# First batch's first 120 rows of scores gathered from an SBUF tile, and blocks of 120, 110, 110 and 108 rows

## The chip, the core and the metric

The kernel runs on one core of a Trainium2 chip. The metric is device microseconds (us) of one execution. Before the change it is 876.28 us, the median of three runs (875.92 to 877.65). The core has the engines that the profile calls PE (TensorE, matrix products; PEld is its weight load), DVE (VectorE), ACT (ScalarE), POOL (GpSimd) and SP (SyncE), which here issues every DMA. SBUF is the on-chip memory, PSUM the banks that PE writes to, DRAM the memory that DMAs reach outside the core.

## The reference

Attention in which the heads are mixed before and after the softmax, followed by a feed-forward layer:

```
q, k, v: (4 batches, 12 heads, 448 rows, 64)   w_pre, w_post: (12, 12)
scores = (q @ k.T) / 8                          # per batch and head, 448 x 448
scores = einsum('bhij,hg->bgij', scores, w_pre) # heads mixed
attn   = exp(scores - max_j);  attn /= (sum_j + 1e-9)
attn   = einsum('bhij,hg->bgij', attn, w_post)  # heads mixed again
x      = (attn @ v) as (1792, 768)
out    = (x@w_in * sigmoid(1.702 * x@w_in)) @ w_out   # w_in 768 x 2048, w_out 2048 x 768
```

## The kernel before

**Attention.** For each batch the scores of a head, 448 rows by 448 columns, are made in four blocks of 112 rows (`QI`). A product (`qk`, L292) leaves one head's block in a PSUM bank, rows on partitions. ACT or DVE copies it to a staging tile `sc` (L327) that holds two heads, and one DMA (L331) sends the pair to the DRAM tensor `sd` of its batch and block, laid out as row, head, column. Six such sends make a block.

The mixing of heads wants the twelve heads of a row on twelve partitions. So the work goes on in 45 steps per batch, a step being ten rows: `gather` (L368) reads ten rows by twelve heads from `sd` into the 120 partitions of a tile `r`, and one product with a block-diagonal matrix `wa` mixes the heads (`mx`, L380). DVE takes the maximum (`nm`, L398), ACT the exponentials and their sum (`e`, L408), POOL and DVE the inverse sum (`rs`, L419 and L424), POOL scales the second mixing matrix (`wr`, L439), PE mixes again and transposes (`pp`, L449), and ACT copies the result to the tile `p` (L503), which holds twelve steps' rows. After twelve steps (the last time nine) `context` multiplies `p` with v (`av`). Batches 0 and 1 do this in float32, batches 2 and 3 with pairs of float16, where a step has two gathers of five rows, each to 60 partitions.

A block of 112 rows does not end where a step ends. The steps 11, 22 and 33 of a batch take rows of two blocks and have a DMA for each. There are four tiles `r`: a gather is issued four steps ahead, when the product of four steps before has freed its tile.

**Feed-forward.** The weights come as 64-bit words, are turned to pairs of float16 on DVE and ACT (L597 to L663, tiles `w`, `w_f`, `w_p`), kept in DRAM (`wd`) and fetched again for each of 32 units (`wt`, L676). The products are `h` (L688) and `po` (L726). They can begin when the first batch's attention is done.

**What sets the order.** The start is written out: six loads of q and k, three of the mixing matrices, then the twelve products of block 0. Of this block the first 64 rows of each pair are sent first, the gathers of the steps 0 to 3 follow, and then the other 48 rows. Its staging tiles are borrowed from places that other tiles use later (`sc`, `g`, `acc`). Everything behind that is ordered by a planner (`add`, `run_all`): a list of tasks with engines, durations, due times and the buffers that they take, from which the order on each engine is written out when the program is built. Each engine, SP too, works through its own list strictly in order. The lines `free.update`, `lanes` and `READY` tell the planner when the engines and the first gathers are free. A DMA's completion is counted on one of eight semaphores in turn, so the ninth DMA waits until the first has landed.

Of the kernel before, what the change touches and what calls it, by code (L numbers as in the profile page):

```python
# [9 lines left out]
F32 = mybir.dt.float32  # L10
# [9 lines left out]
B, H, S, D = 4, 12, 448, 64  # L20
QK16 = (False, False, True, True)
MIX16 = (False, False, True, True)
# [3 lines left out]
GI = 10  # L26
GPB = -(-S // GI)
GPC = 12
CI = GI * GPC
NCH = -(-S // CI)  # L30
QI = 112
KG = GI * H
HI = GI // 2
GAP = 64
# [10 lines left out]
def attention_then_feed_forward(ctx, tc, q, k, v, w_pre, w_post, w_in, w_out, out):  # L45
# [223 lines left out]
        return i0, min(CI, S - i0)  # L269

    def block(c):
        return c * QI, QI

    sd = {}
    for b in range(B):
        for c in range(NCH):
            shape, kind = ([H, 2, S], F16) if MIX16[b] else ([H, S], F32)
            sd[b, c] = dram.tile([block(c)[1]] + shape, kind, name=f"sd_{b}_{c}", tag=f"sd_{b}_{c}")

# [46 lines left out]
        n = block(c)[1]  # L326
        (nc.scalar.copy if eng == "A" else nc.vector.tensor_copy)(t[:n, x, :], two[x][:n, :S])  # L327

    def send_scores(b, c, pr, t, lo=0, hi=QI):
        hi = min(hi, block(c)[1])  # L330
        nc.sync.dma_start(out=sd[b, c][lo:hi, 2 * pr:2 * pr + 2, :], in_=t[lo:hi])  # L331


    def blocks_of(g):
        i0, n = rows_of(g)
        return range(i0 // QI, (i0 + n - 1) // QI + 1)

    def rows_of(g):
        return g * GI, min(GI, S - g * GI)
# [12 lines left out]
    def gather(i):  # L352
        b, g = steps[i]
        i0, n = rows_of(g)
        if MIX16[b]:
            t = flow.tile([128, 2, S], F16, name=f"r_{i}", tag="r", bufs=NRB)
            form = "i h t j -> (i h) t j"
        else:
            t = flow.tile([KG, S], F32, name=f"r_{i}", tag="r", bufs=NRB)
            form = "i h j -> (i h) j"  # L360
        for first, last, at in halves(i):
            if MIX16[b] and g % 2:
                at = GAP - at
            for c in blocks_of(g):
                lo, hi = max(i0 + first, c * QI), min(i0 + last, c * QI + QI)
                if lo < hi:
                    at_lo = at + (lo - i0 - first) * H
                    nc.sync.dma_start(  # L368
                        out=t[at_lo:at_lo + (hi - lo) * H],
                        in_=sd[b, c][lo - c * QI:hi - c * QI].rearrange(form),  # L370
                    )
        row["r", i] = t

    def mix(i):
# [115 lines left out]
    def mixed_to(i):  # L490
        b, g = steps[i]
        n = rows_of(g)[1]
        c, off = g // GPC, (g % GPC) * GI
        if off == 0:
            shape, kind = ([CP, 2, NR, H, CI], F16) if POST16[b] else ([CP, NR, H, CI], F32)
            st["p", b, c] = mixed.tile(shape, kind, name=f"p_{b}_{c}", tag="p")
        p = st["p", b, c]
        if not POST16[b]:
            return p.rearrange("p r h i -> p (r h) i")[:, :, off:off + n]
        return p.rearrange("p t r h i -> p t (r h) i")[:, :, :, off:off + n]  # L500
# [462 lines left out]
        )  # L963

    tags = [("gen", 8)]*3
    homes = [("sc", 3), ("g", 2), ("sc", 3), ("g", 2), ("sc", 3), ("acc", 1)]
    kept = []
    FRONT = 64
    for pr in range(NPAIR):
        two = scores(0, 0, pr, tags[pr % 3])  # L970
        kept.append(scores_home(0, 0, pr, homes[pr]))
        for x in range(2):
            keep_scores(0, 0, x, kept[pr], two, "AD"[x])
        send_scores(0, 0, pr, kept[pr], 0, FRONT)
    nc.vector.tensor_tensor(
        w_mix,
        wrep[:, 0, :].unsqueeze(1).to_broadcast([KG, GI, H]),
# [2 lines left out]
    )  # L980
    mixing(0)
    mixing_pair()
    for i in range(AHEAD):
        gather(i)
    for pr in range(NPAIR):
        send_scores(0, 0, pr, kept[pr], FRONT)


    free.update({"PE": 12.7, "A": 13.3, "D": 16.1, "G": 3.0, "SP": 20.5})
    DMA["free"] = 22.2  # L990
    lanes.extend([19.0, 19.7, 20.4, 21.1, 21.6, 22.2, 22.7, 23.3, 23.8, 24.4])
    READY, LATER = [19.0, 19.7, 20.4, 21.1], 24.4
    held["sc"] = [21.6, 22.7, 23.8]
    held["gen"] = [12.0, 12.2, 12.4, 12.6, 12.8, 12.9, 13.2, 13.5]
    held["g"], held["acc"] = [22.2, 23.3], [24.4]
    r_home = {i: [] for i in range(N)}
    held["r"] = [r_home[i] for i in range(AHEAD)]
    e_home = {i: [] for i in range(N)}
    p_home = {(b, c): [] for b in range(B) for c in range(NCH)}
    x_home = {b: [] for b in range(B)}  # L1000
    acc_home = {b: [] for b in range(B)}
# [198 lines left out]
    for b in range(B):  # L1200
        for c in range(NCH):
            if (b, c) == (0, 0):
                continue
            base = GPB * b + c * QI // GI
            for pr in range(NPAIR):
                x = base - (18 if c == NCH - 1 else 17) + 2 * pr if c else base - 11 + pr
                if b == 0 and (c == 1 or (0, c, pr) in NEAR):
                    x = 0
                x -= (2 if c else 1) * (pr % 2) * (b > 0 or c > 1)
                at_scores.setdefault(max(x, 0), []).append((b, c, pr))  # L1210
# [18 lines left out]
    for i in range(N):  # L1229
        if i + AHEAD < N:  # L1230
            b, g = steps[i + AHEAD]
            n = i + AHEAD
            gathers[n] = add("SP", 0.8 if MIX16[b] else 0.4, lambda n=n: gather(n), [j for c in blocks_of(g) for j in sends.get((b, c), [])], i,
                             size=0.229, takes=[("r", r_home[n])], behind=gathers.get(n - 1))
            if (g + 1) * GI > FRONT and n < GPC:
                gathers[n]["from"] = LATER
        step_tasks(i)
        for what, b, x, *name in at.pop(i, []):
            if what == "whole-kq":
                for n in range(THIRDS):  # L1240
                    for m in "kq":
                        inputs[m, b, n] = whole_load(m, b, n, x + 4 * n)
            elif what == "whole-v":
                loads = [whole_load("v", b, n, x + 2 * n) for n in range(THIRDS)]
                inputs.update({("v", b, n): j for n, j in enumerate(loads)})
                size_tasks("v", b, loads, x + 2, [in_home["v", b, n] for n in range(THIRDS)])
            elif what == "size":
                both = [staged_load(name[0], b, n, "a", x + n) for n in range(THIRDS)]
                size_tasks(name[0], b, [j for j, _ in both], x + 2, [h for _, h in both])
            elif what == "split":  # L1250
                split_tasks(name[0], b, x)
                if name[0] == "q":
                    mixers[b] = add("D", 0.3, lambda b=b: mixing(b), [sized["k", b], sized["q", b], split], x)
            else:
                conversion_tasks(b % 2, b // 2, x)
        for b, c, pr in at_scores.pop(i, []):
            score_tasks(b, c, pr, i)
        b, g = steps[i]
        if g == GPB - 1 or g % GPC == GPC - 1:
            context_tasks(b, g // GPC, i)  # L1260
# [116 lines left out]
```

## Time and profile before

| what | value |
|---|---|
| median of three runs | 876.28 us (875.92 to 877.65) |
| the profiled execution | 875.12 us, span 873.4 us from first to last instruction |
| PE, DVE, ACT, POOL busy | 96%, 73%, 70%, 39% of the span |
| mean granted clock of PE | 0.992 of full speed |
| DMA | 195.64 MB on SP's queue; 225 GB/s on the mean |

The profile is of one execution. Busy time is the time that instructions of an engine ran; a wait is told with what ended it. The windows view gives, for a stretch of the span, the busy time of each engine with the number of its instructions, the clock that PE was granted, the mean busy share of the core's 16 DMA engines and the GB/s that they moved. A share a little above 1 means that packets of one engine overlapped. In the timeline, neighbouring instructions of one group are merged: "x4" are four, and the second number is the time from the first's start to the last's end. A product in float32 is two instructions or more, so one `mx` reads "x2".

### The profile page before, as it was taken

Reading aid. Unit: us, or ns where it says so; the run is one execution under the profiler, and the core shown is the slowest. Engines: PE = TensorE matmul, PEld = TensorE weight load, DVE = VectorE, ACT = ScalarE, POOL = GpSimd, SP = SyncE. Lnnn points to the kernel's source line nnn. Section 1 sums busy time; section 2 is a strip of 40 time slices with the busy share of each in tenths; the row PEclk is TensorE's granted clock in tenths of the full one; section 3 lists DMA queues with packets and bytes.
Section 4 is the critical chain, followed back from the end, with each engine's and each line's share of the span. In section 5 each row is a group of like instructions: output and inputs, shape, how many; then the busy total and the mean of one; then the engine's idle time right before and its main releaser. Section 6 shows DMA issues by size and latency. Waiting matters only on the chain. (4 is left out here: it accounts for less than half of the span.)

```text
span 873.4 us, 20042 instructions
## 1 busy us (share of the span) xinstructions
PE 840.4 (96%) x7300; PEld 515.2 (59%) x7300; DVE 633.3 (73%) x1493; ACT 615.5 (70%) x1373; POOL 340.2 (39%) x529
## 2 busy tenths in 40 slices
PE   8869999999999999989999989999999999999998
PEld 4546756666576666645656546655656566555554
DVE  3657786997979999999878968779786863332323
ACT  4778888896887897967797777677776764324432
POOL 0212332231215632585457634545455553204332
PEclk9989999999999999999999999999999999999999
DMA  7998999999998997777787576587563423252322
GB/s 242 298 288 272 348 297 305 324 341 320 317 341 273 302 315 224 242 225 270 246 278 229 171 252 193 160 231 224 163 202 105 160 80 110 88 189 77 145 86 87
DMA packets 68375, 196.92 MB, mean 225 GB/s; under 512 B 9684, under 2 KB 34516, under 8 KB 68276
## 3 DMA queue, kind: packets, MB, share of 16 engines
q1 hardware_dynamic: 68276, 195.64, 69.4%
q8 instruction: 58, 0.95, 0.4%
q14 instruction: 41, 0.34, 0.1%
HBM read 138.98 MB, written 56.62 MB: 224 GB/s over the span
## 5 line engine op out<-in xcount | busy, mean ns | idle before, releaser
L688 PE MATMUL h<-x,wt 128*128 128x448 f16 x1152 | 246.1, 353 | 0.0
L726 PE MATMUL po<-g,wt 128*128 128x448 f16 x1152 | 240.1, 354 | 3.9 <-ACT e L408 2.9
L726 PEld LDWEIGHTS <-wt 128*128 128x128 f16 x1152 | 110.9, 98 | 101.2 <-issue 7.8
L688 PEld LDWEIGHTS <-wt 128*128 128x128 f16 x1152 | 108.7, 98 | 102.0 <-issue 14.8
L419 POOL TENSOR_SCALAR rs<-sm 120x1 f32<-120x1 f32 (+1 forms) x180 | 52.0, 289 | 275.2 <-ACT e L408 269.3
L398 DVE TENSOR_REDUCE nm<-mx 120x1 f32<-120x448 f32 (+1 forms) x180 | 110.2, 615 | 25.1 <-PE mx L380 15.2
L472 POOL TENSOR_TENSOR a<-w,a 124x448 f16<-124x448 f32 (+1 forms) x90 | 96.1, 1067 | 45.9 <-POOL rs L419 14.5
L449 PEld LDWEIGHTS pp<-wr,e 120*112 120x112 f32 x720 | 84.6, 177 | 36.8 <-issue 19.0
L754 POOL TENSOR_TENSOR acc<-acc,pt 128x448 f32<-128x448 f32 x56 | 65.4, 1169 | 103.9 <-ACT pt L748 96.9
L707 DVE SCALAR_TENSOR_TENSOR th<-th,h 128x448 f32<-128x448 f32 x64 | 39.4, 617 | 86.5 <-ACT th L703 85.7
L380 PE MATMUL mx<-r,wa 120*120 120x448 f32 x180 | 85.3, 564 | 11.0 <-DMA r<-sd 10.0
L449 PE MATMUL pp<-wr,e 120*112 120x120 f32 x720 | 90.4, 269 | 5.1 <-POOL wr L439 4.0
L750 DVE SCALAR_TENSOR_TENSOR acc<-po,ct,acc 128x448 f32<-128x448 f32 x112 | 75.5, 678 | 17.9 <-PE po L726 17.5
L408 ACT ACTIVATE e<-mx,nm,c 124x448 f32<-124x448 f32 (+1 forms) x90 | 65.4, 728 | 24.9 <-DVE nm L400 20.9
L458 POOL TENSOR_SCALAR w<-e,rs 124x448 f32<-124x448 f32 (+1 forms) x90 | 63.5, 706 | 40.4 <-DVE rs L424 29.0
L466 ACT ACTIVATE a<-e,rs 124x448 f16<-124x448 f32 (+1 forms) x90 | 60.3, 672 | 14.7 <-DVE rs L424 14.6
L408 ACT ACTIVATE e<-mx,nm 120x448 f32<-120x448 f32 (+1 forms) x90 | 57.2, 636 | 17.1 <-DVE nm L398 12.8
L748 ACT ACTIVATE pt<-po,ct 128x448 f32<-128x448 f32 x56 | 35.4, 635 | 46.5 <-PE po L726 46.0
L511 DVE TENSOR_TENSOR p<-pp,p 112x480 f16<-112x480 f32 (+1 forms) x90 | 58.2, 648 | 13.7 <-ACT p L507 13.5
L703 ACT ACTIVATE th<-h,ct 128x448 f32<-128x448 f32 x64 | 40.5, 633 | 35.9 <-PE h L688 35.6
L485 PE MATMUL pp<-wp,a 124*112 124x120 f16 x360 | 63.5, 220 | 1.9 <-ACT e L408 1.1
L507 ACT CAST p<-pp 112x480 f16<-112x480 f32 (+1 forms) x90 | 50.6, 562 | 20.4 <-PE pp L487 19.3
(144 smaller groups left out, 1499.0 us busy)
## 6 DMA issues: line engine op xcount, KB each, us to landing
wt<-wd SPq DMA_DIRECT2D x64, 768.0 KB
sd<-sc SPq DMA_DIRECT2D x90, 392.0 KB
r<-sd SPq DMA_DIRECT2D x170, 105.0 KB
r<-sd SPq DMA_DIRECT2D x82, 210.0 KB
w<-in_moe_w_in_dram SPq DMA_DIRECT2D x24, 512.0 KB
w<-in_moe_w_out_dram SPq DMA_DIRECT2D x24, 512.0 KB
wd<-w_p SPq DMA_DIRECT2D x16, 768.0 KB
out_dram<-acc SPq DMA_DIRECT2D x24, 224.0 KB
```

Of the source, the lines that this page charges most:

```text
L380: nc.tensor.matmul(mx[:K, :S], st["wa"][:K, :K], r[:K, :], start=True, stop=True)
L398: nc.vector.tensor_reduce(nm[:K], row["mx", i][:K, :S], axis=AX.X, op=ALU.max, negate=True)
L408: nc.scalar.activation(e[:K], row.pop(("mx", i))[:K, :S], AF.Exp, bias=row.pop(("nm", i))[:K, 0:1], scale=st["c", b][:K, 0:1] if MIX16[b] ...
L449: nc.tensor.matmul(pp[:CP, jc * w:(jc + 1) * w], e[:K, jc * CP:(jc + 1) * CP], columns(i, wr), start=True, stop=True,)
L458: nc.gpsimd.tensor_scalar(w[:K], e[:K], row["rs", i][:K, 0:1], 1.0, op0=ALU.mult, op1=ALU.mult)
L466: nc.scalar.activation(a1[:K], row["e", i][:K], AF.Copy, scale=row["rs", i][:K, 0:1])
L472: nc.gpsimd.tensor_tensor(a2[:K], row.pop(("w", i))[:K], row["a1", i][:K], op=ALU.subtract)
L485: nc.tensor.matmul(o, a1[:K, js], columns(i, wp1), start=True, stop=False)
L688: nc.tensor.matmul(h, w[:, i, c, fc * 128:(fc + 1) * 128], x[:, j, c, :], start=(n == 0), stop=(n == len(terms) - 1),)
L726: nc.tensor.matmul(po, w[:, j, fc, e * 128:(e + 1) * 128], g[:, i, fc, :], start=(n == 0), stop=(n == len(terms) - 1),)
L750: nc.vector.scalar_tensor_tensor(a, po, c, a, op0=ALU.mult, op1=ALU.add)
L754: nc.gpsimd.tensor_tensor(a, a, st.pop(("pt", u, e)), op=ALU.add)
```

## The change

The tile `near`, 120 partitions by 12 heads by 448 columns, takes the copies of the first batch's block 0, which is now 120 rows long. Nothing of it goes to DRAM. The first twelve steps gather from `near`: step g takes the rows g, g+12, g+24 and so on, ten rows from ten partitions, so the rows of a step are not neighbours any more, and `mixed_to` puts a step's results in every twelfth column of `p`. `near` is of the kind `p`, of which there are two. All batches have blocks of 120, 110, 110 and 108 rows, which begin and end where steps do, so no step has rows of two blocks. The front and late parts of the first block's sends are gone, and the borrowed staging tiles with them. The planner's opening numbers are others.

```
@@ -28,7 +28,8 @@
 GPC = 12
 CI = GI * GPC
 NCH = -(-S // CI)
-QI = 112
+BLOCKS = ((0, 120), (120, 110), (230, 110), (340, 108))
+QI = 120
 KG = GI * H
 HI = GI // 2
 GAP = 64
@@ -269,11 +270,11 @@
         return i0, min(CI, S - i0)
 
     def block(c):
-        return c * QI, QI
+        return BLOCKS[c]
 
     sd = {}
     for b in range(B):
-        for c in range(NCH):
+        for c in range(b == 0, NCH):
             shape, kind = ([H, 2, S], F16) if MIX16[b] else ([H, S], F32)
             sd[b, c] = dram.tile([block(c)[1]] + shape, kind, name=f"sd_{b}_{c}", tag=f"sd_{b}_{c}")
 
@@ -326,14 +327,13 @@
         n = block(c)[1]
         (nc.scalar.copy if eng == "A" else nc.vector.tensor_copy)(t[:n, x, :], two[x][:n, :S])
 
-    def send_scores(b, c, pr, t, lo=0, hi=QI):
-        hi = min(hi, block(c)[1])
-        nc.sync.dma_start(out=sd[b, c][lo:hi, 2 * pr:2 * pr + 2, :], in_=t[lo:hi])
-
-
-    def blocks_of(g):
-        i0, n = rows_of(g)
-        return range(i0 // QI, (i0 + n - 1) // QI + 1)
+    def send_scores(b, c, pr, t):
+        n = block(c)[1]
+        nc.sync.dma_start(out=sd[b, c][:, 2 * pr:2 * pr + 2, :], in_=t[:n])
+
+
+    def block_of(g):
+        return max(c for c in range(NCH) if BLOCKS[c][0] <= g * GI)
 
     def rows_of(g):
         return g * GI, min(GI, S - g * GI)
@@ -361,14 +361,15 @@
         for first, last, at in halves(i):
             if MIX16[b] and g % 2:
                 at = GAP - at
-            for c in blocks_of(g):
-                lo, hi = max(i0 + first, c * QI), min(i0 + last, c * QI + QI)
-                if lo < hi:
-                    at_lo = at + (lo - i0 - first) * H
-                    nc.sync.dma_start(
-                        out=t[at_lo:at_lo + (hi - lo) * H],
-                        in_=sd[b, c][lo - c * QI:hi - c * QI].rearrange(form),
-                    )
+            c = block_of(g)
+            lo = i0 - BLOCKS[c][0]
+            if (b, c) == (0, 0):
+                nc.sync.dma_start(out=t, in_=st["near"][g::GPC])
+            else:
+                nc.sync.dma_start(
+                    out=t[at:at + (last - first) * H],
+                    in_=sd[b, c][lo + first:lo + last].rearrange(form),
+                )
         row["r", i] = t
 
     def mix(i):
@@ -495,6 +496,8 @@
             shape, kind = ([CP, 2, NR, H, CI], F16) if POST16[b] else ([CP, NR, H, CI], F32)
             st["p", b, c] = mixed.tile(shape, kind, name=f"p_{b}_{c}", tag="p")
         p = st["p", b, c]
+        if (b, c) == (0, 0):
+            return p.rearrange("p r h i -> p (r h) i")[:, :, g::GPC]
         if not POST16[b]:
             return p.rearrange("p r h i -> p (r h) i")[:, :, off:off + n]
         return p.rearrange("p t r h i -> p t (r h) i")[:, :, :, off:off + n]
@@ -963,15 +966,13 @@
         )
 
     tags = [("gen", 8)]*3
-    homes = [("sc", 3), ("g", 2), ("sc", 3), ("g", 2), ("sc", 3), ("acc", 1)]
-    kept = []
-    FRONT = 64
+    near = st["near"] = mixed.tile([CI, H, S], F32, name="near", tag="p")
     for pr in range(NPAIR):
         two = scores(0, 0, pr, tags[pr % 3])
-        kept.append(scores_home(0, 0, pr, homes[pr]))
         for x in range(2):
-            keep_scores(0, 0, x, kept[pr], two, "AD"[x])
-        send_scores(0, 0, pr, kept[pr], 0, FRONT)
+            (nc.scalar.copy if x == 0 else nc.vector.tensor_copy)(near[:, 2 * pr + x, :], two[x][:CI, :S])
+    for i in range(AHEAD):
+        gather(i)
     nc.vector.tensor_tensor(
         w_mix,
         wrep[:, 0, :].unsqueeze(1).to_broadcast([KG, GI, H]),
@@ -980,22 +981,18 @@
     )
     mixing(0)
     mixing_pair()
-    for i in range(AHEAD):
-        gather(i)
-    for pr in range(NPAIR):
-        send_scores(0, 0, pr, kept[pr], FRONT)
-
-
-    free.update({"PE": 12.7, "A": 13.3, "D": 16.1, "G": 3.0, "SP": 20.5})
-    DMA["free"] = 22.2
-    lanes.extend([19.0, 19.7, 20.4, 21.1, 21.6, 22.2, 22.7, 23.3, 23.8, 24.4])
-    READY, LATER = [19.0, 19.7, 20.4, 21.1], 24.4
-    held["sc"] = [21.6, 22.7, 23.8]
+
+
+    free.update({"PE": 12.5, "A": 13.3, "D": 15.8, "G": 3.0, "SP": 15.6})
+    DMA["free"] = 17.4
+    lanes.extend([15.9, 16.4, 16.9, 17.4])
+    READY = lanes[:]
     held["gen"] = [12.0, 12.2, 12.4, 12.6, 12.8, 12.9, 13.2, 13.5]
-    held["g"], held["acc"] = [22.2, 23.3], [24.4]
     r_home = {i: [] for i in range(N)}
     held["r"] = [r_home[i] for i in range(AHEAD)]
     e_home = {i: [] for i in range(N)}
+    near_home = []
+    held["p"] = [near_home]
     p_home = {(b, c): [] for b in range(B) for c in range(NCH)}
     x_home = {b: [] for b in range(B)}
     acc_home = {b: [] for b in range(B)}
@@ -1201,7 +1198,7 @@
         for c in range(NCH):
             if (b, c) == (0, 0):
                 continue
-            base = GPB * b + c * QI // GI
+            base = GPB * b + BLOCKS[c][0] // GI
             for pr in range(NPAIR):
                 x = base - (18 if c == NCH - 1 else 17) + 2 * pr if c else base - 11 + pr
                 if b == 0 and (c == 1 or (0, c, pr) in NEAR):
@@ -1230,10 +1227,10 @@
         if i + AHEAD < N:
             b, g = steps[i + AHEAD]
             n = i + AHEAD
-            gathers[n] = add("SP", 0.8 if MIX16[b] else 0.4, lambda n=n: gather(n), [j for c in blocks_of(g) for j in sends.get((b, c), [])], i,
+            gathers[n] = add("SP", 0.8 if MIX16[b] else 0.4, lambda n=n: gather(n), sends.get((b, block_of(g)), []), i,
                              size=0.229, takes=[("r", r_home[n])], behind=gathers.get(n - 1))
-            if (g + 1) * GI > FRONT and n < GPC:
-                gathers[n]["from"] = LATER
+            if n < GPC:
+                near_home.append(gathers[n])
         step_tasks(i)
         for what, b, x, *name in at.pop(i, []):
             if what == "whole-kq":
```

SP's list at the start, as it stood before. Here `sd_0_0` is the block 0 of batch 0 in DRAM and `r_0` the tile of step 0:

```order
L331 DMA sd_0_0_97<-sc_0_0_5_208 64x896
L368 DMA r_0_222<-sd_0_0_97 120x448
L368 DMA r_1_224<-sd_0_0_97 120x448
L368 DMA r_2_226<-sd_0_0_97 120x448
L368 DMA r_3_228<-sd_0_0_97 120x448
L331 DMA sd_0_0_97<-sc_0_0_0_168 48x896
```

And as it stands now:

```order
L921 DMA wall_75<-in_w_post_dram 128x144
L367 DMA r_0_200<-near_163 120x1x448
L367 DMA r_1_202<-near_163 120x1x448
L367 DMA r_2_204<-near_163 120x1x448
L367 DMA r_3_206<-near_163 120x1x448
L600 DMA w0_0_64_0_243<-in_moe_w_in_dram 128x1024
L367 DMA r_4_257<-near_163 120x1x448
```

The twelve sends of block 0 are gone, and the first load of weights stands right behind the first four gathers.

SP's list where the first gathers of block 1 stand, before (`sd_0_1` is block 1, `w1_0` a weight load, `vf` a load of v):

```order
L331 DMA sd_0_1_98<-sc_0_1_5_279 112x896
L597 DMA w1_0_64_0_561<-in_moe_w_out_dram 128x1024
L331 DMA sd_0_2_99<-sc_0_2_0_304 112x896
L143 DMA vf2_0_588<-in_v_dram 112x1024
L368 DMA r_11_599<-sd_0_0_97 24x448
L368 DMA r_11_599<-sd_0_1_98 96x448
L368 DMA r_12_602<-sd_0_1_98 120x448
L368 DMA r_13_604<-sd_0_1_98 120x448
L368 DMA r_14_608<-sd_0_1_98 120x448
L331 DMA sd_0_2_99<-sc_0_2_1_323 112x896
L663 DMA wd0_0_113<-w0_0_p_606 128x3072
L368 DMA r_15_631<-sd_0_1_98 120x448
```

And now:

```order
L332 DMA sd_0_1_97<-sc_0_1_5_286 110x896
L600 DMA w1_0_64_0_509<-in_moe_w_out_dram 128x1024
L332 DMA sd_0_2_98<-sc_0_2_0_333 110x896
L144 DMA vf2_0_542<-in_v_dram 112x1024
L369 DMA r_12_560<-sd_0_1_97 120x448
L369 DMA r_13_562<-sd_0_1_97 120x448
L369 DMA r_14_565<-sd_0_1_97 120x448
L369 DMA r_15_573<-sd_0_1_97 120x448
L332 DMA sd_0_2_98<-sc_0_2_1_391 110x896
L600 DMA w1_0_64_1_610<-in_moe_w_out_dram 128x1024
L369 DMA r_16_625<-sd_0_1_97 120x448
```

The first step that needs block 1 is now step 12 and was step 11; the DMAs ahead of it are the same four, and behind step 15's gather a send and a load stand ahead of step 16's.

PE's list at the same place, before:

```order
L449 MATMUL pp_9_555<-wr_9_553,e_9_532 112x120 x4
L449 MATMUL pp_10_577<-wr_10_573,e_10_564 112x120 x4
L122 MATMUL sums_0_586<-w0_0_m_299,ones_77 128x3
L380 MATMUL mx_11_626<-r_11_599,wa_213 120x448
L380 MATMUL mx_12_629<-r_12_602,wa_213 120x448
```

And now:

```order
L381 MATMUL mx_11_524<-r_11_451,wa_209 120x448
L123 MATMUL sums_0_535<-w0_0_m_244,ones_77 128x3
L450 MATMUL pp_8_544<-wr_8_540,e_8_520 112x120 x4
L450 MATMUL pp_9_581<-wr_9_575,e_9_551 112x120 x4
L450 MATMUL pp_10_592<-wr_10_589,e_10_569 112x120 x4
L381 MATMUL mx_12_612<-r_12_560,wa_209 120x448
L450 MATMUL pp_11_618<-wr_11_615,e_11_600 112x120 x4
```

Step 11's first mixing now stands ahead of the second mixings of the steps 8 to 10, and ahead of block 1's first gather.

## Rows read from the trace of the kernel before

**Rows 1.** The page: span; busy time, share and instructions of each engine.

```profile
span 873.4 us, 20042 instructions
PE 840.4 (96%) x7300; PEld 515.2 (59%) x7300; DVE 633.3 (73%) x1493; ACT 615.5 (70%) x1373; POOL 340.2 (39%) x529
```

**Rows 2.** Windows: stretch, length, busy by engine, PE's clock, DMA share, GB/s.

```profile
core 0: us, PE busy (x) PEld busy (x) DVE busy (x) ACT busy (x) POOL busy (x), PEclk, DMA share, GB/s
40.00:50.00 10.00, 5.74 (x42) 4.50 (x40) 5.21 (x18) 9.44 (x25) 2.61 (x8) 1.00 1.03 346
55.00:60.00 5.00, 4.96 (x16) 2.56 (x15) 3.65 (x14) 2.66 (x8) 1.11 (x4) 0.67 0.57 177
80.00:85.00 5.00, 5.00 (x30) 3.36 (x29) 4.87 (x9) 4.80 (x11) 1.94 (x3) 1.00 0.51 105
85.00:100.00 15.00, 13.56 (x108) 9.34 (x108) 13.01 (x44) 13.53 (x34) 5.11 (x13) 1.00 1.00 353
100.00:150.00 50.00, 48.79 (x381) 33.44 (x379) 35.81 (x90) 40.98 (x105) 13.33 (x36) 1.00 0.98 304
600.00:700.00 100.00, 100.00 (x1106) 60.57 (x1104) 76.99 (x173) 72.48 (x155) 53.03 (x81) 1.00 0.54 170
```

**Rows 3.** PE's waits from 0 to 60 us: total, times, longest.

```profile
PE mx L380 <- DMA r<-sd: 8.5, 5, 5.6
```

**Rows 4.** Timeline, 11 to 20 us: start, length, engine, line, what; in brackets the wait.

```profile
11.54 1.38 DVE L327 COPY sc<-qk 112x448 f32<-112x448 f32 x2 [0.92 <-PE qk L292]
16.71 1.73 SPq L368 DMA_DIRECT2D r<-sd  x4
19.39 0.98 PE L380 MATMUL mx<-r,wa 120*120 120x448 f32 x2 [1.13 <-DMA r<-sd]
```

**Rows 5.** The DMA view: packets, SP's queue, and issues by size.

```profile
DMA packets 68375, 196.92 MB, mean 225 GB/s; under 512 B 9684, under 2 KB 34516, under 8 KB 68276
q1 hardware_dynamic: 68276, 195.64, 69.4%
...
r<-sd SPq DMA_DIRECT2D x170, 105.0 KB
r<-sd SPq DMA_DIRECT2D x82, 210.0 KB
...
gap_rep<-in_w_pre_dram SPq DMA_DIRECT2D x2, 2.8 KB
wrep<-in_w_pre_dram SPq DMA_DIRECT2D x1, 5.6 KB
```

**Rows 6.** Timeline, 40 to 60 us.

```profile
40.16 1.67 PE L380 MATMUL mx<-r,wa 120*120 120x448 f32 x4
53.32 3.31 PE L380 MATMUL mx<-r,wa 120*120 120x448 f32 x4 [5.63 <-DMA r<-sd]
54.19 0.32 PEld L380 LDWEIGHTS mx<-r,wa 120*120 120x120 f32 x1 [0.42 <-DMA r<-sd]
56.71 2.53 PE L380 MATMUL mx<-r,wa 120*120 120x448 f32 x4
```

**Rows 7.** Timeline: gathers of the steps 35, 45, 60, and their products.

```profile
107.55 1.92 SPq L368 DMA_DIRECT2D r<-sd  x2
113.50 0.98 PE L380 MATMUL mx<-r,wa 120*120 120x448 f32 x2 [1.00 <-DMA r<-sd]
...
137.57 0.33 SPq L368 DMA_DIRECT2D r<-sd  x1
144.80 0.92 PE L380 MATMUL mx<-r,wa 120*120 120x448 f32 x2
...
174.53 0.37 SPq L368 DMA_DIRECT2D r<-sd  x1
189.64 0.92 PE L380 MATMUL mx<-r,wa 120*120 120x448 f32 x2
```

**Rows 8.** Timeline: one copy of a step's result to `p` on ACT.

```profile
27.53 0.57 ACT L503 COPY p<-pp 112x480 f32<-112x480 f32 x1
```

## The prediction

> **What bounds the kernel now.** I read the page's busy times first, then windows over the span, then PE's waits, the timeline around the longest of them, and the DMA view. PE is busy 840.4 of 873.4 us [rows 1] and full from 600 to 700 us [rows 2], where the feed-forward products run: a us that PE loses early is not found again, and one that it does not lose is won. The early part is where it loses: 8.5 us of waits for gathers before 60 us, 5.6 us of them in one [rows 3]. There PE has nothing left before the first gather of block 1, which waits for that block's six sends. The DMA share in the same stretch is 1.03, and it stays at 0.98 to 1.00 from 85 to 150 us, in which PE is busy 62.4 of 65 us [rows 2]. Two things are near their limit there, PE and the DMA engines, and the change touches the second.
>
> The pace of one DMA engine follows from SP's queue: 195.64 MB in 69.4% of 16 times 873.4 us are 20.2 kB per busy us [rows 5] (kB are 1000 bytes here). It is hardly a matter of load: 304 GB/s at a share of 0.98 and 170 at 0.54 are 19.4 and 19.7 [rows 2]. So an engine does not get faster when others have less to do, and a transfer lasts as long as the engine with the largest part of it.
>
> **How transfers are divided.** 598 DMAs stand in the program, and 9684 packets are under 512 B [rows 5]. 480 of these are the 48 B rows of `wrep` and `gap_rep` (two copies of 120 rows, four of 60). The other 9204 I take for one completion packet of each part of a DMA. With 16 parts each they would be 9568, so 364 are missing. They come out exactly if a DMA is cut into the greatest number of equal parts, up to 16, that divides its row counts on both sides: 15 for the 252 gathers of 60 or 120 rows, 12 for the 14 short pieces that steps at a block's end need (24, 36, 72 or 12 rows), 10 for each `wrep`, 5 for each `gap_rep`, 16 for all others, the sends of 112, 64 and 48 rows among them: 252 + 56 + 12 + 44 = 364. By this a send of 110 rows has 11 parts, one of 108 has 12, one of 120 has 15, and a gather from `near`, ten source rows to 120, has 10. The Trainium skill, "DMA: Bandwidth & Descriptors", section "Why a DMA increments its semaphore by 16 and not by 1", states this rule, and that the parts go to the lowest-numbered engines; the trace agrees with the count of 9204, and which engines it were is in no row here. With 16 parts for everything the sum below would have 550 kB in place of 740 and step 12 would be 9.4 us earlier, bounded by PE.
>
> **The change part by part.** The sum is made against the profiled execution, 875.12 us (span 873.4, 1.7 around it); the median of the runs is 1.2 above that.
>
> *The start.* Block 0's last copy ends at 11.54 + 1.38 = 12.9 us, but the first gather is issued at 16.71, after the sends have landed [rows 4]. Now it follows the copies: about 13.0. From issue to the product were 2.68 us. A gather has 215 kB; its largest part grows from 14.3 to 21.5 kB, 0.36 us more. First product: 16.0, against 19.39, 3.4 us earlier. PE is free by then: 20 score products stand ahead of it in its list, where 28 did.
>
> *To step 12.* From its first gather to the gather of step 12, SP's list has 12 gathers from `near` (21.5 kB on the fullest engine each), 7 sends of 110 rows (394 kB by 11: 35.8), 4 weight loads (524 kB by 16: 32.8), 3 loads of v (28.7) and the gather itself (14.3): 258 + 251 + 131 + 86 + 14 = 740 kB. Before it was 643 kB with more bytes in all (9.9 MB against 8.8, without step 12's gather): what the 12 sends of block 0 set free, the uneven parts take back. At 20.2 kB per us 740 kB last 36.6 us. With 1.94 us of issue and landing (2.68 less the 0.71 of a 14.3 kB part) step 12 has its rows at 13.0 + 1.94 + 36.6 = 51.6. Slots and data are there in time for SP to keep the queue filled. Before, the products of steps 11 and 12 were the four instructions from 53.32, so step 12's began at 54.97, its rows landed at about 54.2 [rows 6]. 3.4 us are won. No row shows a DMA from SBUF to SBUF; the bounds are the paces of 85 to 100 us, 353/16 = 22.1, and of 100 to 150 us, 19.0 [rows 2]: 48.4 to 53.9, so 1.1 to 6.6 us won. I take 20.2, the mean over the whole queue.
>
> *From step 12 to step 45*, the first of batch 1. The list has the same kinds of transfer, 19 sends among them, but those cost the fullest engine 7 times 35.8, 6 times 32.3 and 6 times 28.7 kB in place of 19 times 25.1: 617 against 476 kB. All together 1822 kB against 1686. Step 35's rows came 5.9 us after the gather's issue and PE waited 1.0 us for them; step 45's were issued 7.2 us before their product [rows 7]. So they landed at about 143.5, 1.3 us early: no cushion to speak of. 1686 kB took 143.5 - 54.2 = 89.3 us, and in it lie two lulls, 55 to 60 us (0.57: 2.1 us) and 80 to 85 us (0.51: 2.4 us) [rows 2]; without them the pace is 19.9. The first lull, SP behind gathers whose tiles PE had not freed, I let go, since a send and a load now stand between; the second, four tiny loads, stays. After: 51.6 + 1822/19.9 + 2.4 = 145.6. With its head start PE would ask for these rows at 144.8 - 3.4 = 141.4. They are 4.2 us late, and the gain of 3.4 turns into a loss of 0.8. Bounds: at 22.1 and from 48.4 they land at 133.2 and nothing is late; at 19.0 and from 53.9 at 152.2, 7.4 us later than PE asked for them before.
>
> *After step 45* the uneven sends go on, +40 kB to step 60 and +109 kB to step 75, 2.0 and 5.4 us on the fullest engine. But step 60's gather is issued 15.1 us before its product [rows 7], 9 us more than it needs. I cost this at nothing; without that cover it is up to 7.4 us.
>
> *The rest.* Twelve copies to `p` (0.57 us each, [rows 8]) write every twelfth column. ACT is busy 9.44 of 10 us from 40 to 50 [rows 2]. At nothing, since PE waits for DMAs then; twice as long would be 6.8 us, of which 1 to 3 could show. The matrix products are the same in number, the planner's interleaving reaches step 60 with the same feed-forward products as before, and its small shifts later (eight copies from DVE to ACT) I take as 2 us either way. PE's clock was at half from about 53 to 59 us, after the wait of 5.6 us. There the eight `mx` instructions took 3.31 + 2.53 us; four at full clock took 1.67 [rows 6], so it cost 2.5 us. I leave it in: PE still waits before step 12.
>
> Sum: 875.12 + 0.8 = 875.9; with the 1.2 between the profile and the median, 877.
>
> **Rivals.**
> *Faster: the head start stays.* Transfers from `near` are quicker than those from DRAM, so the fullest engine is not late at step 45, and the clock stays up after a shorter wait. For it: what stands in `near` need not be read from DRAM. Against it: the fuller engines. 3.4 + 2.5 = 5.9 us won: 870.4. The Trainium skill, same page, section "Where 436 GB/s comes from", has DMAs within SBUF bound at 435 GB/s and those with DRAM at 358; by an estimate from that page the twelve gathers would take 9.5 us of an engine in place of 12.8 and step 12 come 3.3 us earlier still. No row here shows it.
> *Slower: uneven parts bind up to step 75.* One mechanism, the sends of 110 and 108 rows. It decides when step 45's rows land later than about 148 us; then SP also issues the gathers behind them late and their cover of 9 us goes. With the bound of 152.2, 7.4 us are lost: 876.3 + 7.4 = 884. For it: PE already waited at step 35, the DMA share is 1. Against it: the cover from step 60 on.
> *The change does not do what it says*: the first product does not come earlier, since PE is behind; I give it nothing, PE sits idle before it now.
>
> **How the numbers follow.** About 0.2% (1.75 us) is what a measurement of this kernel can tell from no change: below 874.5 is faster, above 878.0 slower. Head start given back (877, from 874 to 880): 0.40, of it 0.05 faster, 0.20 the same, 0.15 slower. Head start stays: 0.30, of it 0.28 faster, 0.02 the same. Uneven parts bind: 0.30, of it 0.29 slower, 0.01 the same. Together 0.33, 0.23, 0.44. The range from 868 to 887 holds the 870.4 and the 884 with the 2 to 3 us of the smaller unknowns; the likeliest case's own range is 874 to 880.
>
> **What would show it.** The first `mx` at 16 us; step 12's at about 52 and a shorter wait before it; the number of packets under 512 B at 8930 (574 DMAs cut as above, 8450, and 480); waits of `mx` for gathers between 85 and 145 us, some 4 us, where step 35's 1.0 is the longest now; step 45's product near 145.6. I am wrong if PE does not wait there (faster), or if it waits for gathers beyond step 60 (slower).

## The result: 7.4 us slower

The changed kernel takes 883.48 us (median of 4 runs, 882.95 to 884.46), the kernel before 876.1 beside it: ratio 1.0087, 95% interval 1.0063 to 1.0112. The prediction's 877 was the case in which the head start is given back; the time that came is the one that its slower rival gave, 884, and 883.48 lies within the range of 868 to 887. The profiled execution took 883.2 us.

The first lines of the page of the changed kernel, then its lines of packets and of SP's queue:

```profile
span 881.4 us, 20006 instructions
PE 847.2 (96%) x7300; PEld 517.0 (59%) x7300; DVE 625.2 (71%) x1481; ACT 623.9 (71%) x1384; POOL 335.4 (38%) x533
...
DMA packets 66900, 194.33 MB, mean 220 GB/s; under 512 B 8930, under 2 KB 33762, under 8 KB 66802
...
q1 hardware_dynamic: 66802, 193.05, 67.4%
```

Against [rows 1] the span is 8.0 us longer, and PE's busy time takes 6.8 of it with the same 7300 matmuls; its idle time is 34.2 us where it was 33.0. Equal work that takes longer is a slower clock: the mean granted clock of the execution is 0.986, against 0.992 before, 12.3 us of full clock lost against 7.0 (one less the clock, times the span). So some 5 of the 8.0 us between these two profiles stand in no list of waits. Two executions are few for that, though: over all timed executions the same product is 11.0 us for the change (4 executions) and 9.3 and 9.0 for the kernel before (25 and 26), so on the mean the half clock makes up 2 of the 7.4 us. The bytes are fewer than in [rows 5], and the packets under 512 B are the 8930 of the prediction.

Windows of the changed kernel, columns as in [rows 2]:

```profile
40.00:50.00 10.00, 6.22 (x30) 4.03 (x29) 4.30 (x14) 9.87 (x25) 2.20 (x6) 0.84 0.85 278
55.00:60.00 5.00, 4.30 (x58) 3.41 (x58) 4.68 (x18) 3.99 (x11) 1.44 (x5) 1.00 0.89 319
80.00:85.00 5.00, 3.59 (x14) 1.75 (x14) 4.78 (x16) 4.53 (x12) 0.75 (x3) 1.00 0.68 190
85.00:100.00 15.00, 11.54 (x54) 6.77 (x56) 10.07 (x31) 10.18 (x25) 2.89 (x9) 0.77 0.83 286
100.00:150.00 50.00, 49.60 (x416) 34.32 (x412) 35.22 (x89) 41.99 (x107) 12.77 (x37) 1.00 0.96 306
600.00:700.00 100.00, 100.00 (x1116) 60.63 (x1115) 78.41 (x176) 70.93 (x151) 50.66 (x79) 1.00 0.55 177
```

From 85 to 100 us PE does 54 matmuls where it did 108, at a clock of 0.77, while the DMA share fell from 1.00 to 0.83 and the rate from 353 to 286 GB/s. A lower share looks like room. It is a mean over 16 engines, though; the last section counts how many packets were under way at a time.

The timeline of the changed kernel, at the places of [rows 4], [rows 6] and [rows 7]; the row at 144.54 is the product of step 45:

```profile
12.88 3.31 SPq L367 DMA_DIRECT2D r<-near  x4
15.85 0.98 PE L381 MATMUL mx<-r,wa 120*120 120x448 f32 x2 [0.71 <-DVE sc L328]
...
47.97 1.07 PE L450 MATMUL pp<-wr,e 120*112 120x120 f32 x8 [1.69 <-POOL wr L440]
49.90 1.94 PE L450 MATMUL pp<-wr,e 120*112 120x120 f32 x8 [0.85 <-POOL wr L440]
51.63 1.70 PE L381 MATMUL mx<-r,wa 120*120 120x448 f32 x2
...
144.54 0.98 PE L381 MATMUL mx<-r,wa 120*120 120x448 f32 x2
```

The first product comes at 15.85 and step 12's at 51.63, 3.3 us earlier than before. The 5.63 us wait of [rows 6] is gone, but not because PE no longer waits: smaller waits for `wr`, which follows from ACT's `e`, stand in its place. By aligning the two traces at points where PE has done the same work, the changed kernel is 3.4 us ahead at step 18, 1.9 behind at step 30, 1.1 at step 42, 2.8 at step 48, 6.1 at step 53 and 8.0 at the end. The two lists order their work differently, so such points are rough: by the start of a step's own product it is 0.3 us ahead at step 45 and 1.7 behind at step 60 (191.30 against 189.64).

Three places show how time goes, the timeline of the changed kernel again, PE, ACT and SP's issues:

```profile
29.70 0.90 SPq L600 DMA_DIRECT2D w<-in_moe_w_in_dram  x1
36.80 0.66 ACT L607 ACTIVATE w_f<-w 128x512 f32<-128x512 f32 x1 [3.56 <-DMA w<-in_moe_w_in_dram]
...
75.14 1.76 PE L293 MATMUL qk<-kf,qf 64*108 64x448 f32 x8
76.97 0.67 ACT L607 ACTIVATE w_f<-w 128x512 f32<-128x512 f32 x1 [2.07 <-DMA w<-in_moe_w_in_dram]
80.60 1.01 PE L381 MATMUL mx<-r,wa 120*120 120x448 f32 x2 [0.70 <-ACT e L409]
82.03 1.07 PE L450 MATMUL pp<-wr,e 120*112 120x120 f32 x8 [0.42 <-POOL wr L440]
88.46 1.82 PE L381 MATMUL mx<-r,wa 120*120 120x448 f32 x2 [3.85 <-ACT p L506]
90.21 3.33 PE L293 MATMUL qk<-kf,qf 64*108 64x448 f32 x8
...
145.55 0.32 SPq L369 DMA_DIRECT2D r<-sd  x1
146.83 0.67 ACT L607 ACTIVATE w_f<-w 128x512 f32<-128x512 f32 x1 [1.60 <-DMA w<-in_moe_w_out_dram]
```

ACT works in order. While it stands before a conversion whose weights have not landed (2.07 us at 76.97, 3.56 at 36.80 for the load issued at 29.70, and 1.60 at 146.83), its exponentials and copies wait behind it, and PE then waits for `e` and for `wr`, which is made from `e`'s sums. After the stall of 3.85 us the clock is at half: eight `qk` take 3.33 us, which took 1.76 at 75.14. The gather issued at 145.55 is that of step 49, whose product waits for it until 154.08 (shown with the even sends below).

### The profile page after: what moved, and what is told of

Read it like the earlier page. It is cut to its first block, busy times and chain, and to the rows that moved or that the text cites. A ratio compares the mean times of both kernels' runs of the same rounds, so it can differ in the third digit from the quotient of the medians.

```text
span 881.4 us, 20006 instructions
## 1 busy us (share of the span) xinstructions
PE 847.2 (96%) x7300; PEld 517.0 (59%) x7300; DVE 625.2 (71%) x1481; ACT 623.9 (71%) x1384; POOL 335.4 (38%) x533
## 2 busy tenths in 40 slices
DMA packets 66900, 194.33 MB, mean 220 GB/s; under 512 B 8930, under 2 KB 33762, under 8 KB 66802
## 4 chain that ended last, share of the span: by engine, by line
PE 76%; DVE 8%; DMA 8%; ACT 4%; issue 2%; POOL 1%; SPq 1%; ACTq 0%; POOLq 0%; DVEq 0%
PE po L729 22%; PE h L691 22%; PE pp L450 6%; PE mx L381 5%; PE av L539 3%; PE av L528 3%; PE mx L394 3%; PE qk L293 2%; PE qk L303 2%; DMA w<-in_moe_w_in_dram 2%; PE pp L486 2%; PE pp L488 2%; PE pp L487 2%; DMA w<-in_moe_w_out_dram 2%; DMA ka<-in_k_dram 1%
## 5 line engine op out<-in xcount | busy, mean ns | idle before, releaser
L420 POOL TENSOR_SCALAR rs<-sm 120x1 f32<-120x1 f32 (+1 forms) x180 | 49.1, 273 | 266.6 <-ACT e L409 259.9
L473 POOL TENSOR_TENSOR a<-w,a 124x448 f16<-124x448 f32 (+1 forms) x90 | 96.3, 1070 | 53.7 <-ACT a L467 20.1
L450 PEld LDWEIGHTS pp<-wr,e 120*112 120x112 f32 x720 | 86.6, 180 | 39.3 <-issue 20.7
L450 PE MATMUL pp<-wr,e 120*112 120x120 f32 x720 | 93.2, 273 | 6.0 <-POOL wr L440 5.4
L753 DVE SCALAR_TENSOR_TENSOR acc<-po,ct,acc 128x448 f32<-128x448 f32 x109 | 73.1, 676 | 16.6 <-PE po L729 16.2
L751 ACT ACTIVATE pt<-po,ct 128x448 f32<-128x448 f32 x59 | 37.3, 634 | 45.2 <-PE po L729 44.7
L440 POOL TENSOR_SCALAR wr<-wp,rs 120x120 f32<-120x120 f32 (+1 forms) x90 | 43.1, 480 | 65.4 <-DVE rs L425 41.5
```

What stands on the lines that cost most here:

```text
L450: nc.tensor.matmul(pp[:CP, jc * w:(jc + 1) * w], e[:K, jc * CP:(jc + 1) * CP], columns(i, wr), start=True, stop=True,)
L473: nc.gpsimd.tensor_tensor(a2[:K], row.pop(("w", i))[:K], row["a1", i][:K], op=ALU.subtract)
L753: nc.vector.scalar_tensor_tensor(a, po, c, a, op0=ALU.mult, op1=ALU.add)
```

## The experiments

Theory A: the sends of 110 and 108 rows, cut into 11 and 12 parts, make SP's queue late, and later waits on ACT and the half clock are how that arrives at PE. Rivals: the strided copies to `p`, the new order of the lists, the layout of the blocks as such. Each run below was timed against the kernel before on the same chip, 876.67 us in the first set, 875.93 in the second.

**Even sends** (`e1_even`). The changed kernel with sends of 16 equal parts:

```
-BLOCKS = ((0, 120), (120, 110), (230, 110), (340, 108))
-QI = 120
+BLOCKS = ((0, 128), (120, 112), (230, 112), (336, 112))
+QI = 128
...
-            base = GPB * b + BLOCKS[c][0] // GI
+            base = GPB * b - (-BLOCKS[c][0] // GI)
```

> The changed kernel with blocks of 128, 112, 112 and 112 rows (starts 0, 120, 230, 336), so that every send has a row count that 16 divides; each engine's list is word for word that of the changed kernel, but for the row counts. Theory A, the uneven parts of the sends of 110 and 108 rows make the DMAs late and cost most of what was lost from step 23 on: 874 to 878 us. Theory B, the twelve strided copies to p on ACT: unchanged, 882 to 885. Theory C, the new order of the lists: unchanged, 882 to 885.

872.83 us (10 runs), ratio 0.996, 0.9933 to 0.9987: 10.7 us better than the change by the medians (11.1 by the ratios), with the same lists, and faster than the kernel before; it is 1.2 us below the interval that theory A gave it. The page of this variant:

```profile
span 871.6 us, 20006 instructions
PE 840.6 (96%) x7300; PEld 512.6 (59%) x7300; DVE 627.7 (72%) x1481; ACT 624.3 (72%) x1384; POOL 337.3 (39%) x533
```

ACT's waits for weights from 0 to 200 us (total, times, longest), here:

```profile
ACT w_f L607 <- DMA w<-in_moe_w_in_dram: 2.5, 3, 2.0
ACT w_f L607 <- DMA w<-in_moe_w_out_dram: 0.5, 1, 0.5
```

and the same waits in the changed kernel:

```profile
ACT w_f L607 <- DMA w<-in_moe_w_in_dram: 7.8, 4, 3.6
ACT w_f L607 <- DMA w<-in_moe_w_out_dram: 3.0, 3, 1.6
```

PE's busy time is that of the kernel before again, with a clock of 0.992, and of 10.8 us of ACT's waits for weights 3.0 are left (the kernel before has 6.4). At points of the same work it is 1.1 us ahead of the changed kernel at step 21, 3.2 at step 24, 4.2 at step 42, 7.7 at step 51, 8.5 at step 80, and 9.8 from step 130 on. The stretch to step 24 is that of the conversion at 76.97; here PE goes through it without a wait. PE's stall after it is no work of the uneven sends, though: the even variant has it too, at the same product and as long, and there its name is a gather. PE's timeline of the even variant:

```profile
76.64 0.92 PE L381 MATMUL mx<-r,wa 120*120 120x448 f32 x2
77.40 0.98 PE L450 MATMUL pp<-wr,e 120*112 120x120 f32 x8
79.79 1.67 PE L381 MATMUL mx<-r,wa 120*120 120x448 f32 x4
85.38 0.98 PE L381 MATMUL mx<-r,wa 120*120 120x448 f32 x2 [3.92 <-DMA r<-sd]
...
148.00 0.98 PE L381 MATMUL mx<-r,wa 120*120 120x448 f32 x2 [0.62 <-DMA r<-sd]
149.59 2.04 PE L528 MATMUL av<-p,vf 112*64 112x88 f32 x48 [0.61 <-ACT p L506]
```

The same two instructions as the last rows, of the changed kernel:

```profile
154.08 0.98 PE L381 MATMUL mx<-r,wa 120*120 120x448 f32 x2 [1.43 <-DMA r<-sd]
155.72 3.65 PE L528 MATMUL av<-p,vf 112*64 112x88 f32 x48 [0.65 <-ACT p L506]
```

There the waits are 0.85 us longer and the half clock that comes with them costs 1.61 on one group of matmuls.

**Dense copies** (`e2_dense_p`). The changed kernel writes its twelve copies side by side, and leaves out putting the rows of the output back in order:

```
-        if (b, c) == (0, 0):
-            return p.rearrange("p r h i -> p (r h) i")[:, :, g::GPC]
```

> The changed kernel with the results of the first twelve steps written to neighbouring columns of p, as before; the output then has the first 120 rows of the first batch in another order. Lists are the same. Theory B: the copies take 0.57 us again instead of 1.0, 12 x 0.43 = 5 us less on ACT, the waits for POOL's wr between 44 and 52 us go, 878 to 880 us. Theory A: 2 to 3 us are won before step 12 and given back to late DMAs behind it, 881 to 884. Theory C: 882 to 885.

881.87 us (10 runs), ratio 1.006, 1.0034 to 1.0087: 1.6 us less than the change, and the two intervals overlap. One such copy on ACT, strided in the changed kernel and dense here:

```profile
21.92 1.00 ACT L506 COPY p<-pp 112x480 f32<-112x480 f32 x1
```
```profile
22.70 0.56 ACT L504 COPY p<-pp 112x480 f32<-112x480 f32 x1
```

The stride costs 0.44 us in this pair. All twelve run on ACT and take 12.1 us together where the dense ones take 6.8: 5.3 us of its time, of which 1.6 by the medians arrive at the end, and that is not clear of the noise.

**Dense copies on even sends** (`e4_even_dense`). Both edits, and the two operations that write `x` put the rows of the first block back in order.

> Both of the first two: blocks of 128, 112, 112 and 112 rows, dense copies to p, and the order of rows restored where x is written (four instructions of ACT and DVE in place of twelve copies). Theory A with B as a smaller part: the head start stays, 871 to 875 us. Theory C: 878 to 884.

873.84 us (10 runs), ratio 0.9966, 0.9943 to 0.9988: nothing won over the even sends alone.

**Uneven blocks alone** (`e3_blocks_alone`). The kernel before with blocks of 120, 110, 110 and 108 rows; the first 120 rows still go through DRAM, sent in two pieces:

```
-QI = 112
+BLOCKS = ((0, 120), (120, 110), (230, 110), (340, 108))
+QI = 120
...
-        return c * QI, QI
+        return BLOCKS[c]
...
```

> The kernel before with blocks of 120, 110, 110 and 108 rows and nothing else: block 0 of the first batch still goes to DRAM and back. Theory A: slower than before by the uneven parts of all sends, without the head start: 880 to 886 us. Theories B and C (what is lost comes from the tile near, its strided copies or the order around it): as before, 874 to 878.

894.9 us (4 runs), ratio 1.0191, 1.0138 to 1.0244: 18 us by the medians, more than theory A gave. PE's waits for gathers, 0 to 200 us:

```profile
PE mx L381 <- DMA r<-sd: 13.6, 9, 4.7
```

Of these 8.6 us come behind 60 us, where the kernel before has 1.4, so here waits for gathers show where the prediction had looked for them. But 18 us are more than the sends gave back in the first run, so something else had come with the blocks; the next set takes it apart.

**Two transfers per send** (`e5_two_sends`). The changed kernel with its own blocks, each send in two:

```
-        nc.sync.dma_start(out=sd[b, c][:, 2 * pr:2 * pr + 2, :], in_=t[:n])
+        cut = {120: 112, 110: 80, 108: 96}[n]
+        for lo, hi in ((0, cut), (cut, n)):
+            nc.sync.dma_start(out=sd[b, c][lo:hi, 2 * pr:2 * pr + 2, :], in_=t[lo:hi])
```

> The changed kernel with its own blocks of 120, 110, 110 and 108 rows, but each send to the DRAM tile split in two: the first 80 of 110 rows (16 parts of 5 rows) and the other 30 (15 parts of 2), the first 96 of 108 (16 parts of 6) and the other 12 (12 parts of 1), the first 112 of 120 and the other 8. The fullest engine gets 7 rows of a send of 110 or 108 where it had 10 or 9; every other instruction and its order is that of the changed kernel, only the sends are issued twice. Theory A (the parts of the sends are what the even blocks gave back, 10.7 us): 871 to 878 us. Rival B (the number of rows in a block, that is where rows lie in the DRAM tile and which send a gather waits for): 881 to 886. Rival C (a transfer more per send costs more than its even parts give): 884 to 895.

875.52 us (10 runs), ratio 1.0014, 0.9986 to 1.0042: by the medians 8.0 of the 10.7 us are back, by the ratios 6.4 of 11.1, with the blocks unchanged and 90 transfers more. Rivals B and C are out. Its page, and below it the same row of the even sends:

```profile
DMA packets 68407, 194.34 MB, mean 221 GB/s; under 512 B 10436, under 2 KB 35268, under 8 KB 68308
```
```profile
DMA packets 67590, 195.54 MB, mean 224 GB/s; under 512 B 9284, under 2 KB 34116, under 8 KB 67492
```

The prediction's rule of parts can be held against both. The 90 sends (18 of 120 rows, 48 of 110, 24 of 108) have 15, 11 and 12 parts in the changed kernel, 1086 in all; 16 each in the even variant, 354 more, and 9284 less 8930 is 354; 24, 31 and 28 when cut in two, 1506 more, and 10436 less 8930 is 1506. So theory A stands for the larger part of the loss. The 2.7 us to the even sends (4.7 by the ratios) are left open between the added transfers and the blocks.

How the sends make the queue late stands in SP's own waits. Gathers that wait in SP's list for a send to land, 20 to 200 us (total, times, longest), in the kernel before, the change, the even sends and the sends cut in two (a profiled execution of 880.55 us, 5 above its median):

```profile
SPq L368 <- DMA sd<-sc: 5.2, 3, 4.5
```
```profile
SPq L369 <- DMA sd<-sc: 11.3, 5, 3.8
```
```profile
SPq L369 <- DMA sd<-sc: 2.2, 2, 2.0
```
```profile
SPq L371 <- DMA sd<-sc: 4.2, 3, 3.5
```

Whatever stands behind such a gather in SP's list, weight loads among it, is issued later by as much.

**Even sends in the first batch, and in the others** (`e6_even_first`, `e8_even_later`). The block table becomes a function of the batch:

```
+EVEN = ((0, 128), (120, 112), (230, 112), (336, 112))
...
+def blk(b):
+    return EVEN if b == 0 else BLOCKS
...
```

(in the other run `b > 0`).

> The changed kernel with sends of 112 rows (blocks of 128, 112, 112 and 112, as in the even variant) in the first batch alone; the other batches keep 120, 110, 110 and 108. Lists of instructions word for word those of the changed kernel. Theory A in two halves: the even variant was 4.2 us ahead of the changed kernel at step 42, and 9.8 from step 130 on, so the first batch's sends are worth 4 to 6 us and this runs at 877 to 880. Rival D (all of it starts with the first batch, the rest is its later growth): 871 to 875. Rival E (the later batches' sends alone): 882 to 885.

> The changed kernel with sends of 112 rows in every batch but the first, which keeps 110, 110 and 108. Lists of instructions those of the changed kernel. Theory A in two halves: the later batches are worth 5 to 7 us, 876 to 879. Rival D (all of it starts with the first batch): 882 to 885. Rival E (the later batches alone): 871 to 875.

880.75 us (10 runs), ratio 1.0054, 1.0026 to 1.0083, and 877.35 (10 runs), 1.001, 0.9992 to 1.0028. From the ratio of the change these are 2.9 and 6.7 us, 9.6 together of 11.1 for both (1.27%): some two thirds of the loss come from the sends of the batches behind the first, and neither half is all of it, since the interval of the even variant lies below both. The shares are rough: the interval with the first batch even overlaps with that of the change. The first is 0.75 us above the interval that theory A gave it. The waits follow the sends: ACT waits 4.0 us for `in_moe_w_in` when the first batch is even and 7.3 when it is not, and for `in_moe_w_out`, which is loaded later, 1.7 and 0.6.

**Even, aligned blocks in the kernel before** (`e7_before_even`). The table of the even variant put into the kernel of `e3_blocks_alone`:

> The kernel before with the blocks of the even variant (128, 112, 112 and 112 rows that start at multiples of ten) and nothing else of the change: the first 120 rows still go through DRAM. Its lists of instructions are those of the kernel before with blocks of 120, 110, 110 and 108, which took 894.9 us. Theory A (uneven parts cost there as much as in the changed kernel, or more): 872 to 886. Rival F (the 18 us came from the other order and from gathers that need one block alone): 890 to 896.

882.89 us (5 runs), ratio 1.0072, 1.0041 to 1.0103. With this run the change can be taken apart:

| us | first 120 rows through DRAM | in `near` | `near` is worth |
|---|---|---|---|
| sends of 112 and 128 rows | 882.9 | 872.8 | -10.1 |
| sends of 110 and 108 rows | 894.9 | 883.5 | -11.4 |
| uneven parts cost | 12.0 | 10.7 | |

And the kernel before, whose blocks of 112 rows are cut through by steps, stands at 876: to make blocks begin at a step costs 7 us, by this table of blocks. The change so falls into three: +7 for the blocks, some -10.7 for `near` and the planner's order that comes with it, some +11.3 for the uneven parts. That these add up to the measured time is no further evidence, since they are all differences of the same five medians. The medians stem from sets whose kernel before differs by up to 0.7 us.

Why aligned blocks cost 7 us is not settled. This table sends 16 rows of each batch twice, which by an estimate from the 20.2 kB per us of the prediction (six sends with one row of 3.58 kB more on the fullest engine) is 1.1 us of an engine per batch. The planner makes another list (a step needs one block's sends where it needed two), and in its trace PE waits for gathers at the first steps of the second batch as it does not before, as this row of PE's timeline has it:

```profile
150.79 2.49 PE L381 MATMUL mx<-r,wa 120*120 120x448 f32 x6 [3.69 <-DMA r<-sd]
```

Its waits for gathers behind 60 us are 7.2 us, not much below the 8.6 with uneven parts, so most of those in `e3_blocks_alone` came with the aligned blocks. No run put the old order on the new blocks.

## Why the prediction was right or wrong

As a whole, 883.48 lies outside 874 to 880, the range of the case that I held likeliest, and inside 868 to 887 because that range takes in the slower rival. Where a landing is given below, it is the last of the sixteen completions that the trace holds for that gather.

*The start*: right. 15.85 for 16.0, and the gathers issue at 12.88 for 13.0.

*How transfers are divided*: right. 8930 came out to the packet, and the counts of the variants follow the same rule. The Trainium skill, "DMA: Bandwidth & Descriptors", section "Why a DMA increments its semaphore by 16 and not by 1", has a transfer go to the largest number of engines, up to 16, that divides the slowest dimension of both sides; the trace agrees with 354 and 1506 packets more. What fewer engines cost, these runs measured: 6.4 to 8.0 us for sends of 120, 110 and 108 rows against the same rows in two pieces. One sum of that paragraph is wrong: with 16 parts for everything the 740 kB would be 565, not 550, and step 12 would come 8.7 us earlier, not 9.4.

*To step 12*: the number for the product was right by luck, 51.63 for 51.6. The rows landed at 50.85 (53.71 before), 0.8 us earlier than the sum had them (its 2.68 less 0.71 are 1.97, not 1.94, which the 51.6 has right), and the product did not wait for them; PE was held by `wr` and `e` behind ACT, which was busy 9.87 of 10 us and had waited 3.56 us for a weight load.

*From step 12 to step 45*: the size was right, the form not. I had a head start of 3.4 us turn into a loss of 0.8; by work done it is a loss of 1.1 at step 42, and step 45's rows landed at 144.40, just ahead of its product at 144.54, where I had 145.6 for them. Before, they landed at 141.89, not at the 143.5 that I had worked out. But of the 4 us of waits of `mx` for gathers between 85 and 145 us none stands in the trace under that name. The one of 3.85 us is put down to `p`, whose copy ended at 88.36, but step 26's gather landed at 88.32, so both held PE alike; and since the even variant stalls there as long, this one is not the price of uneven parts. The even variant gains 3.1 us from step 21 to step 42, and that is what the uneven sends cost here. The others are ACT's, for weights. I had followed one kind of passenger in SP's queue. Weight loads ride in the same queue.

*After step 45*: this is the step that failed. "I cost this at nothing", for the cover of 9 us at step 60; it cost 6.9 us, from 1.1 behind at step 42 to 8.0 at the end. I had read the cover at step 60 and let it stand for all steps from 45 on. Step 49's gather was issued 8.5 us before its product and still came 1.43 us late (issued at 145.55, landed at 153.95), and the matmuls behind it lost 1.61 us to the half clock. At step 60 the cover holds: after 154 us PE waits for no gather. And it says nothing of a weight conversion at the head of ACT's list, which waited 1.60 us at 146.83. Of the 5.6 us that the even variant gains behind step 42, 3.5 come by step 51. Even sends in the later batches alone gave 6.7 us back, which puts the price on these sends. My slower rival had the cause and the size (884), but its size by luck: its condition, step 45's rows later than about 148, did not come, they landed at 144.40, and its sign, waits for gathers beyond step 60, did not come either.

*The copies to `p`*: the strided ones take 1.00 us for 0.57, inside the bound of twice as long, and of the 1 to 3 us that I let show 1.6 do, not clear of the noise.

*The half clock*: I left 2.5 us of it in and took no more. It is some 5 us more than before between the two profiles, and 2 us more on the mean of all timed executions.

*The faster rival* had `near` worth 5.9 us through faster transfers. `near` is worth 10 to 11 us on equal blocks, more than that rival gave it, but no run shows that faster transfers are the reason: none timed the gathers from `near` apart. The price that neither of us had is the 7 us of the aligned blocks.

## What to carry to other kernels

Before changing the rows of a transfer, ask into how many equal parts, up to 16, the count divides: 112 rows are 16 parts of 7, 110 are 11 of 10, and of the 10.7 us that this kernel lost against even sends, two transfers per send gave 6 to 8 back. When a queue gets later, list everyone who rides in it and who waits for each, since the first to be late need not be the one that waited before. A cover read at one step holds for that step only. And compare PE's busy time, not only its waits, over more than one execution: here stalls came back as half clock.

## What the runs showed of the hardware

- Here the queue with uneven parts shows a lower DMA share, not a higher one. SP's queue from 20 to 200 us, of the kernel before, the change and the even sends, in this order (packets, MB, share):

```profile
q1 hardware_dynamic: 20504, 55.14, 95.8%
```
```profile
q1 hardware_dynamic: 18853, 51.21, 88.5%
```
```profile
q1 hardware_dynamic: 20076, 54.56, 92.5%
```

  Per busy us of an engine these are 20.0, 20.1 and 20.5 kB: the pace is the same. The packets' own times in the traces show where the share went: from 20 to 200 us the number of packets under way was 10, 11 or 12 for 20% of the time in the change, for 3% in the kernel before, 6% with even sends and 8% with the sends cut in two. So in the change some engines stand idle while others work on a send of 11 or 12 parts.
- A copy of 112x480 f32 on ACT whose output is every twelfth column takes 0.98 to 1.06 us, 0.55 to 0.59 when dense.
- After PE's stall of 3.85 us the granted clock from 88 to 94 us is 0.50 in this trace, 1.2 GHz, and the stretch of six us does the work of three. The even variant, with the same stall of 3.92 us, has 0.63 and 0.51 in the two us each from 86 and 88 us and 1.00 from 90 on: how long the clock stays down differs between two kernels with one list.
